# Retention then gated FFN on one core: the two stages interleaved, head pairs on half tiles, decays folded into v and y

## The chip, the core and the metric

The kernel runs on one core of one Trainium2 chip. The core has TensorE (PE, matmuls into PSUM; PEld is its weight load), VectorE (DVE), ScalarE (ACT), GpSimd (POOL) and SyncE (SP). Each runs its own instructions in the order written and waits on semaphores for the others. 16 DMA engines move data; a transfer is issued from the queue of SP, ACT or POOL, and an issue is an instruction like any other there. The metric is the device time of one execution in microseconds (us), lower is better.

## The reference

Batch 4, 8 heads, 768 positions, head size 64; then 3072 tokens of width 512 through an FFN of width 1536. Inputs and output are float32 in DRAM.

```python
gamma = 1.0 - 2.0 ** (-5.0 - np.arange(H))            # one decay per head
for t in range(S):
    state = gamma * state + einsum('bhd,bhe->bhde', k[:, :, t], v[:, :, t])
    y[:, :, t] = scale * einsum('bhd,bhde->bhe', q[:, :, t], state)
x = y.transpose(0, 2, 1, 3).reshape(B * S, H * D)
out = (1 / (1 + exp(-(x @ w_gate)))) * (x @ w_val) @ w_out
```

## The kernel before

It has two stages, one after the other; x stays on chip between them, transposed (features on partitions), in four tiles `xT` of 128 x 3072.

The retention stage loops over head `h`, and inside over batch entry `b`: 32 (head, batch) pairs. `issue_qkv_dma` (L84) loads q, k and v of the next pair with three transfers of 192 KB, issued from POOL, ACT and SP. ACT converts them to bf16 (L138). Six TensorE transposes (L147, L151) and twelve DVE copies make `qT` and `kT` with the 64 features on partitions. Then it walks six chunks of 128 positions. For each: scores `st_p` (L167, contraction over 64), a DVE product with the head's decay mask (L169), two matmuls that add into `yT_p` (L172 from the chunk, L173 from the state), an ACT copy into `xT` (L177), `cross_p` (L180), and a DVE step that decays the state and adds `cross_p` (L183). The state is a 64 x 64 bf16 tile in SBUF. All these work on one head, so they fill half of TensorE's rows or columns. The decay tables of each head are built at the head's start (ACT Exp with DVE and POOL steps).

The weights come in 20 transfers from POOL's queue (L135), two or three per head, converted to bf16 on the way.

The FFN stage loops over six tiles of 512 tokens. Per tile there are 12 pairs of `gate_p` and `val_p` (L199, L203: four matmuls of 512 columns each), a Sigmoid on ACT (L207) and a product on DVE (L208), and then four `out_p` of 12 matmuls each (L213), an ACT copy (L216) and a store from SP (L217).

A scheduler orders the instructions within each stage. PSUM pools of the retention stage are closed before those of the FFN open.

Of the kernel before, what the change touches and what calls it, by code (L numbers as in the profile page):

```python
# [10 lines left out]
F32 = mybir.dt.float32  # L11
BF16 = mybir.dt.bfloat16
I32 = mybir.dt.int32
# [5 lines left out]
def kernel(  # L19
# [15 lines left out]
    NCHUNK = S // C  # L35
    scale = 1.0 / math.sqrt(D)
    KT = D_MODEL // 128
    NFF = D_FF // 128
    MT = N_TOK // 512

    const = ctx.enter_context(tc.tile_pool(name="const", bufs=1))
    ident = const.tile([128, 128], BF16)
    make_identity(nc, ident)

    ii_free = const.tile([128, 128], I32)
    nc.gpsimd.iota(ii_free, pattern=[[1, 128]], base=0, channel_multiplier=-1)
    ii_col = const.tile([D, 128], I32)
    nc.gpsimd.iota(ii_col, pattern=[[1, 128]], base=0, channel_multiplier=0)
    ii_part = const.tile([128, 1], I32)
    nc.gpsimd.iota(ii_part, pattern=[[1, 1]], base=0, channel_multiplier=1)  # L50

    ii_free_f = const.tile([128, 128], F32)
    nc.vector.tensor_copy(ii_free_f, ii_free)
    ii_col_f = const.tile([D, 128], F32)
    nc.vector.tensor_copy(ii_col_f, ii_col)
    ii_part_f = const.tile([128, 1], F32)
    nc.vector.tensor_copy(ii_part_f, ii_part)

    xpool = ctx.enter_context(tc.tile_pool(name="xpool", bufs=1))
    xT_sb = [xpool.tile([128, N_TOK], BF16, tag=f"xT{kk}", name=f"xT{kk}")  # L60
             for kk in range(KT)]

    wpool = ctx.enter_context(tc.tile_pool(name="wpool", bufs=1))

    w_jobs = []
    def load_w_bf16(ap, tagbase, ktiles, width):
        tiles = []
        for kk in range(ktiles):
            tb = wpool.tile([128, width], BF16, tag=f"{tagbase}{kk}", name=f"{tagbase}{kk}")
            w_jobs.append((tb, ap[kk * 128:(kk + 1) * 128, :]))  # L70
            tiles.append(tb)
        return tiles

    wg_sb = load_w_bf16(moe_w_gate, "wg", KT, D_FF)
    wv_sb = load_w_bf16(moe_w_val, "wv", KT, D_FF)
    wo_sb = load_w_bf16(moe_w_out, "wo", NFF, D_MODEL)
    n_jobs = len(w_jobs)
    jobs_per_h = [(n_jobs * (i + 1)) // H - (n_jobs * i) // H for i in range(H)]
    job_idx = 0

    def issue_qkv_dma(attn, bb, hh):
        tfn = attn.tile([C, 3 * D * NCHUNK], F32, tag="qkvF")
        for i, (ap, eng) in enumerate([(q, nc.gpsimd), (k, nc.scalar), (v, nc.sync)]):
            eng.dma_start(  # L84
                out=tfn[:, i * D * NCHUNK:(i + 1) * D * NCHUNK].rearrange("s (c d) -> s c d", c=NCHUNK),
                in_=ap[bb, hh].rearrange("(c s) d -> s c d", c=NCHUNK))
        return tfn

    with tc.tile_pool(name="hmask", bufs=1) as hmask, \
         tc.tile_pool(name="attn", bufs=3) as attn, \  # L90
         tc.tile_pool(name="ps1", bufs=2, space=bass.MemoryType.PSUM) as ps1:
      tf_next = issue_qkv_dma(attn, 0, 0)
      for h in range(H):
          gamma = 1.0 - 2.0 ** (-5.0 - h)
          lg = math.log(gamma)
          cross_decay = gamma ** C

          b128 = hmask.tile([128, 1], F32, tag="b128")
          b64 = hmask.tile([D, 1], F32, tag="b64")

          mask_T = hmask.tile([128, 128], BF16, tag="mask")
          mtmp = hmask.tile([128, 128], F32, tag="mtmp")
          nc.vector.memset(b128, math.log(scale))
          nc.scalar.activation(mtmp, ii_free_f, AX.Exp, scale=lg, bias=b128)
          nc.gpsimd.affine_select(mtmp, mtmp, pattern=[[1, 128]], base=0,
                                  channel_multiplier=-1,
                                  compare_op=ALU.is_ge, fill=0.0)
          nc.vector.tensor_copy(mask_T, mtmp)

          lam = hmask.tile([D, S], BF16, tag="lam")  # L110
          ltmp = hmask.tile([D, 128], F32, tag="ltmp")
          nc.vector.memset(b64, math.log(scale) + lg)
          nc.scalar.activation(ltmp, ii_col_f, AX.Exp, scale=lg, bias=b64)
          for c in range(NCHUNK):
              nc.vector.tensor_copy(lam[:, c * C:(c + 1) * C], ltmp)  # L115

          eta = hmask.tile([128, 1], F32, tag="eta")
          nc.vector.memset(b128, (C - 1) * lg)
          nc.scalar.activation(eta, ii_part_f, AX.Exp, scale=-lg, bias=b128)

          xk = h // 2
          xoff = (h % 2) * D

          for b in range(B):
              state = attn.tile([D, D], BF16, tag="state")
              nc.gpsimd.memset(state, 0.0)

              tf = tf_next
              nb, nh = (b + 1, h) if b + 1 < B else (0, h + 1)
              if nh < H:  # L130
                  tf_next = issue_qkv_dma(attn, nb, nh)
              if b == 0:
                  for _ in range(jobs_per_h[h]):
                      tb_w, ap_w = w_jobs[job_idx]
                      nc.gpsimd.dma_start(out=tb_w, in_=ap_w)  # L135
                      job_idx += 1
              tb = attn.tile([C, 3 * D * NCHUNK], BF16, tag="qkvB")
              nc.scalar.activation(tb, tf, AX.Copy)  # L138
              qB = tb[:, 0:D * NCHUNK]
              kB = tb[:, D * NCHUNK:2 * D * NCHUNK]  # L140
              vB = tb[:, 2 * D * NCHUNK:3 * D * NCHUNK]

              qT = attn.tile([D, S], BF16, tag="qT")
              kT = attn.tile([D, S], BF16, tag="kT")
              for c2 in range(NCHUNK // 2):
                  qtp = ps1.tile([C, C], BF16, tag="tp", bufs=2)
                  nc.tensor.transpose(qtp, qB[:, c2 * C:(c2 + 1) * C], ident)  # L147
# [101 lines left out]
```

## Time and profile before

| what | value |
|---|---|
| median of 3 runs | 451.34 us (451.21 to 452.57) |
| profiled execution, span from first to last instruction | 449.5 us |
| TensorE busy | 391.6 us, 87% of the span |
| VectorE busy | 243.7 us, 54% |
| ScalarE busy | 152.7 us, 34% |
| GpSimd busy | 45.7 us, 10% |
| read from DRAM, written to DRAM | 28.31 MB, 6.29 MB |

The page gives no time of the profiled execution besides its span; the span is 1.84 us shorter than the median of the runs. TensorE's busy time counts overlapping matmuls by modelled ends, so 87% is no measure of how full its array is. The shares are averages over two stages that have different limits; the stages are told apart by reading stretches of the trace.

### The profile page before, as it was taken

Reading aid. Unit: us, or ns where it says so; the run is one execution under the profiler, and the core shown is the slowest. Engines: PE = TensorE matmul, PEld = TensorE weight load, DVE = VectorE, ACT = ScalarE, POOL = GpSimd, SP = SyncE. Lnnn points to the kernel's source line nnn. Section 1 sums busy time; section 2 is a strip of 40 time slices with the busy share of each in tenths; the row PEclk is TensorE's granted clock in tenths of the full one; section 3 lists DMA queues with packets and bytes.
Section 4 is the critical chain, followed back from the end, with each engine's and each line's share of the span. In section 5 each row is a group of like instructions: output and inputs, shape, how many; then the busy total and the mean of one; then the engine's idle time right before and its main releaser. Section 6 shows DMA issues by size and latency. Waiting matters only on the chain.

```text
span 449.5 us, 5825 instructions
## 1 busy us (share of the span) xinstructions
PE 391.6 (87%) x1824; PEld 188.0 (42%) x1824; DVE 243.7 (54%) x987; ACT 152.7 (34%) x346; POOL 45.7 (10%) x101
## 2 busy tenths in 40 slices
PE   1797987887896978878878899999999999999996
PEld 0343443443443434434444444444444444444442
DVE  3778787777878787877778634043132141330330
ACT  3333333334343343434242243233232332332321
POOL 5444111101101010111000000000000000000000
PEclk9999999999999999999999999999999999999999
DMA  9999633242423342242200000200200101101002
GB/s 186 225 235 219 137 88 71 58 102 53 105 55 79 79 96 64 64 95 53 53 3 1 1 1 0 77 18 0 95 0 25 71 0 48 47 2 70 23 1 93
DMA packets 58591, 30.26 MB, mean 67 GB/s; under 512 B 51392, under 2 KB 52928, under 8 KB 58560
## 3 DMA queue, kind: packets, MB, share of 16 engines
q0 software_dynamic: 4928, 11.01, 11.1%
q1 hardware_dynamic: 28544, 12.59, 10.6%
q10 hardware_dynamic: 25088, 6.29, 6.7%
q8 instruction: 14, 0.23, 0.2%
q14 instruction: 17, 0.14, 0.1%
HBM read 28.31 MB, written 6.29 MB: 77 GB/s over the span
## 4 chain that ended last, share of the span: by engine, by line
PE 57%; DVE 16%; issue 2%; ACT 1%; POOL 0%; ACTq 0%
PE gate_p L199 14%; PE val_p L203 14%; PE out_p L213 14%; PE yT_p L173 5%; PE st_p L167 4%; PE cross_p L180 3%; PE yT_p L172 3%; DVE qT L149 3%; DVE kT L153 3%; DVE kT L152 3%; DVE q_sc L156 2%; DVE qT L148 2%; DVE st L169 1%; DVE eta_v L158 1%; DVE lam L115 1%
## 5 line engine op out<-in xcount | busy, mean ns | idle before, releaser
L208 DVE TENSOR_TENSOR h<-gate_s,val_p 128x512 bf16<-128x512 f32 x72 | 49.5, 687 | 130.0 <-PE val_p L203 125.1
L177 ACT ACTIVATE xT<-yT_p 64x128 bf16<-64x128 f32 x192 | 51.4, 268 | 154.5 <-PE yT_p L173 154.2
L169 DVE TENSOR_TENSOR st<-st_p,mask_T 128x128 bf16<-128x128 f32 x192 | 55.4, 289 | 41.7 <-PE st_p L167 40.5
L199 PE MATMUL gate_p<-xT,wg 128*128 128x512 bf16 x288 | 74.7, 382 | 0.4 <-ACT xT L177 0.4
L203 PE MATMUL val_p<-xT,wv 128*128 128x512 bf16 x288 | 74.5, 382 | 0.0
L207 ACT ACTIVATE gate_s<-gate_p 128x512 f32<-128x512 f32 x72 | 43.0, 597 | 74.9 <-PE gate_p L199 74.9
L213 PE MATMUL out_p<-wo,h 128*128 128x512 bf16 x288 | 63.1, 379 | 0.0
L172 PE MATMUL yT_p<-st,tb 128*64 128x128 bf16 x192 | 57.8, 301 | 2.3 <-DVE st L169 0.5
L167 PE MATMUL st_p<-qT,kT 64*128 64x128 bf16 x192 | 54.7, 285 | 0.0
L180 PE MATMUL cross_p<-eta_v,tb 128*64 128x64 bf16 x192 | 42.0, 249 | 13.5 <-DVE eta_v L158 13.5
L173 PE MATMUL yT_p<-q_sc,state_new 64*64 64x128 bf16 x160 | 50.0, 313 | 0.0
L147 PE MATMUL qtp<-ident,tb 128*128 128x128 bf16 x96 | 27.6, 287 | 19.6 <-DVE qT L149 10.0
L151 PE MATMUL ktp<-ident,tb 128*128 128x128 bf16 x96 | 27.7, 288 | 18.5 <-DVE kT L153 18.3
L203 PEld LDWEIGHTS <-wv 128*128 128x128 bf16 x288 | 28.4, 99 | 34.6 <-issue 1.1
L199 PEld LDWEIGHTS <-wg 128*128 128x128 bf16 x288 | 28.3, 98 | 34.7 <-issue 1.1
L213 PEld LDWEIGHTS <-h 128*128 128x128 bf16 x288 | 28.2, 98 | 34.0
L138 ACT ACTIVATE tb<-tfn 128x1152 bf16<-128x1152 f32 x32 | 37.1, 1162 | 6.8 <-DMA tfn<-in_q_dram 4.2
L180 PEld LDWEIGHTS <-tb 128*64 128x64 bf16 x192 | 24.4, 128 | 30.4 <-issue 12.0
L183 DVE SCALAR_TENSOR_TENSOR state_new<-state_new,cross_p 64x64 bf16<-64x64 bf16 x160 | 32.4, 203 | 1.6 <-PE yT_p L173 0.8
L216 ACT COPY out_sb<-out_p 128x512 f32<-128x512 f32 x24 | 14.0, 585 | 53.5 <-PE out_p L213 53.5
L172 PEld LDWEIGHTS <-tb 128*64 128x64 bf16 x192 | 27.4, 143 | 10.2 <-DVE st L169 5.9
L84 POOL DMA_DIRECT2D tfn<-in_q_dram x32 | 26.8, 837 | 43.3 <-ACT xT L177 36.4
(40 smaller groups left out, 235.5 us busy)
## 6 DMA issues: line engine op xcount, KB each, us to landing
tfn<-in_k_dram ACTq DMA_DIRECT2D x32, 192.0 KB, 3.9
tfn<-in_v_dram SPq DMA_DIRECT2D x32, 192.0 KB, 3.4
tfn<-in_q_dram POOLq DMA_DIRECT2D x32, 192.0 KB, 4.4
out_dram<-out_sb SPq DMA_DIRECT2D x24, 256.0 KB, 2.0
wg<-in_moe_w_gate_dram POOLq DMA_DIRECT2D x4, 384.0 KB, 8.5
wv<-in_moe_w_val_dram POOLq DMA_DIRECT2D x4, 384.0 KB, 8.5
wo<-in_moe_w_out_dram POOLq DMA_DIRECT2D x12, 128.0 KB, 7.8
```

The lines of the kernel that those rows point to most:

```text
L138: nc.scalar.activation(tb, tf, AX.Copy)
L167: nc.tensor.matmul(st_p, k_dc, q_dc, start=True, stop=True)
L169: nc.vector.tensor_mul(st, st_p, mask_T)
L172: nc.tensor.matmul(yT_p, v_cd, st, start=True, stop=False)
L173: nc.tensor.matmul(yT_p, state, q_sc[:, c * C:(c + 1) * C], start=False, stop=True)
L177: nc.scalar.activation(xT_sb[xk][xoff:xoff + D, col0:col0 + C], yT_p, AX.Copy)
L180: nc.tensor.matmul(cross_p, k_cd, eta_v[:, c * D:(c + 1) * D], start=True, stop=True)
L199: nc.tensor.matmul(gate_p, wg_sb[kk][:, n1 * 128:(n1 + 1) * 128], xT_sb[kk][:, mt * 512:(mt + 1) * 512], start=(kk == 0), stop=(kk == KT - 1))
L203: nc.tensor.matmul(val_p, wv_sb[kk][:, n1 * 128:(n1 + 1) * 128], xT_sb[kk][:, mt * 512:(mt + 1) * 512], start=(kk == 0), stop=(kk == KT - 1))
L207: nc.scalar.activation(gate_s, gate_p, AX.Sigmoid)
L208: nc.vector.tensor_mul(hT[n1], gate_s, val_p)
L213: nc.tensor.matmul(out_p, hT[n1][:, sm * 128:(sm + 1) * 128], wo_sb[n1], start=(n1 == 0), stop=(n1 == NFF - 1))
```

## The change

The kernel is rewritten with its order given by hand. Work is organised by batch entry, and inside it by chunks of 128 positions of all eight heads at once (`load_chunk`: 128 x 8 x 64). q and k are converted to bf16 by the transfer itself and issued from POOL; v stays float32 and is issued from SP.

The decay gamma^(i-j) is split into gamma^-j, multiplied into v by POOL (`scale_v`, table `tabv`), and scale * gamma^i, multiplied into y by DVE (`taby`, the last line of `step_y`). What is between is plain causal attention without decay, so the masks are the same for all heads and the state is a plain sum: `z` adds up in one PSUM bank over the chunks of a batch entry.

Heads are handled in pairs. `step_t` transposes k and q of a chunk (8 matmuls, two heads each) and ACT copies all into SBUF at once. `step_s` makes the scores, 8 matmuls with a contraction of 64: even heads on rows 0 to 63 of the array, odd heads on rows 64 to 127, into two PSUM banks; DVE applies the causal mask to four heads at a time. `step_y` adds to `z` (4 matmuls), reads the masked copy of the earlier state (4 matmuls, not for the first chunk) and adds the products with the scores (8 matmuls into 64 output partitions each, even and odd heads on the two halves of the columns).

The FFN takes 768 tokens of one batch entry: 24 groups `up` (half of the tokens, four matmuls of 384 columns for the gate and four for the value) and 6 groups `down` (12 matmuls of 512 columns). The last loop emits the groups of entry b and between them, at most one after each group, the 18 steps of entry b+1. The steps of entry 0 come ahead of all groups. PSUM is split between five banks of attention, one each, and three that the FFN rotates through (`ff`).

The core of the diff (the removed loops stand in the functions above):

```diff
+    ctx.enter_context(tc.manual_schedule())
...
+    ld = ctx.enter_context(tc.tile_pool(name="ld", bufs=12))
+    at = ctx.enter_context(tc.tile_pool(name="at", bufs=2))
+    ffn = ctx.enter_context(tc.tile_pool(name="ffn", bufs=3))
+    pa = ctx.enter_context(tc.tile_pool(name="pa", bufs=1, space=bass.MemoryType.PSUM))
+    pf = ctx.enter_context(tc.tile_pool(name="pf", bufs=3, space=bass.MemoryType.PSUM))
...
+        vf[b, c] = ld.tile([C, H, D], F32, tag="vf", name="vf", bufs=8)
+        nc.gpsimd.dma_start(out=kn[b, c], in_=k[b, :, rows, :].rearrange("h s d -> s h d"))
+        nc.gpsimd.dma_start(out=qn[b, c], in_=q[b, :, rows, :].rearrange("h s d -> s h d"))
+        nc.sync.dma_start(out=vf[b, c], in_=v[b, :, rows, :].rearrange("h s d -> s h d"))
...
+    def load_gate_val(s):
+        cols = slice(s * 256, (s + 1) * 256)
+        for dst, src in ((wg, moe_w_gate), (wv, moe_w_val)):
+            nc.gpsimd.dma_start(out=dst[:, :, cols],
+                                in_=src.rearrange("(kk p) n -> p kk n", p=128)[:, :, cols])
...
+    def scale_v(b, c):
+        vs[b, c] = ld.tile([C, H, D], BF16, tag="vs", name="vs", bufs=8)
+        nc.gpsimd.tensor_tensor(vs[b, c], vf[b, c],
+                                tabv[:, c, :].unsqueeze(2).to_broadcast([C, H, D]), op=ALU.mult)
+
+    def step_t(b, c):
+        tp = pa.tile([128, 2 * NP, C], BF16, tag="tp", name="tp")
+        for i, src in enumerate((kn[b, c], qn[b, c])):
+            for p in range(NP):
+                nc.tensor.transpose(tp[:, i * NP + p, :],
+                                    src[:, 2 * p:2 * p + 2, :].rearrange("s h d -> s (h d)"), ident)
+        qkT[b, c] = at.tile([128, 2 * NP, C], BF16, tag="qkT", name="qkT")
+        nc.scalar.activation(qkT[b, c], tp, AX.Copy)
+
+    def step_s(b, c):
+        t = qkT[b, c]
...
+        for p in range(NP):
+            nc.tensor.matmul(sA[:, p, :], t[0:D, p, :], t[0:D, NP + p, :], start=True, stop=True)
+            nc.tensor.matmul(sB[:, p, :], t[D:128, p, :], t[D:128, NP + p, :], start=True, stop=True)
...
+        nc.vector.tensor_tensor(stA[b, c], sA, causal4, op=ALU.mult)
+        nc.vector.tensor_tensor(stB[b, c], sB, causal4, op=ALU.mult)
+
+    def step_y(b, c):
...
+                nc.tensor.matmul(zps[b][:, p, :],
+                                 kn[b, c][:, 2 * p:2 * p + 2, :].rearrange("s h d -> s (h d)"),
+                                 vs[b, c][:, 2 * p:2 * p + 2, :].rearrange("s h d -> s (h d)"),
+                                 start=(c == 0 and p == 0), stop=True, skip_group_check=True)
...
+                nc.tensor.matmul(y[:, p, :], zbd[b, c - 1][:, p, :], t[:, NP + p, :],
+                                 start=(p == 0), stop=False, skip_group_check=True)
+        for p in range(NP):
+            nc.tensor.matmul(y[0:D, p, :], vs[b, c][:, 2 * p, :], stA[b, c][:, p, :],
+                             start=(c == 0 and p == 0), stop=True, skip_group_check=True)
+            nc.tensor.matmul(y[D:128, p, :], vs[b, c][:, 2 * p + 1, :], stB[b, c][:, p, :],
+                             start=(c == 0 and p == 0), stop=True, skip_group_check=True)
+        if c < NCH - 1:
+            zbd[b, c] = at.tile([128, NP, C], BF16, tag="zbd", name="zbd")
+            nc.vector.tensor_tensor(zbd[b, c], zps[b], diag4, op=ALU.mult)
+        cols = slice(c * C, (c + 1) * C)
+        nc.vector.tensor_tensor(xT[b][:, :, cols], y, taby[:, :, cols], op=ALU.mult)
+
+    def attention(b):
+        steps = [lambda: step_t(b, 0), lambda: step_s(b, 0)]
+        for c in range(NCH):
+            if c + 1 < NCH:
+                steps.append(lambda c=c: step_t(b, c + 1))
+            steps.append(lambda c=c: step_y(b, c))
+            if c + 1 < NCH:
+                steps.append(lambda c=c: step_s(b, c + 1))
+        return steps
...
+        def up(n1, hf):
+            cols = slice(hf * HALF, (hf + 1) * HALF)
+            ps = []
+            for w in (wg, wv):
+                t = pf.tile([128, 512], F32, tag="ff", name="ff")
+                for kk in range(KT):
+                    nc.tensor.matmul(t[:, 0:HALF], w[:, kk, n1 * 128:(n1 + 1) * 128], xT[b][:, kk, cols],
+                                     start=(kk == 0), stop=(kk == KT - 1))
+                ps.append(t)
+            gs = ffn.tile([128, HALF], F32, tag="gs", name="gs")
+            nc.scalar.activation(gs, ps[0][:, 0:HALF], AX.Sigmoid)
+            nc.vector.tensor_tensor(hT[:, n1, cols], gs, ps[1][:, 0:HALF], op=ALU.mult)
...
+    for s in range(NFF // 2):
+        load_gate_val(s)
+    for s in range(4):
+        load_out(s)
+    for c in range(NCH):
+        scale_v(0, c)
+    for c in range(NCH):
+        load_chunk(1, c)
+    for step in attention(0):
+        step()
+    for b in range(B):
+        groups = ffn_groups(b)
+        steps = attention(b + 1) if b + 1 < B else []
...
+        for i, g in enumerate(groups):
+            g()
+            upto = -(-len(steps) * (i + 1) // len(groups))
+            while done < min(upto, len(steps)):
+                steps[done]()
+                done += 1
```

Three places in the new order matter below. The first is POOL's queue in the first part of the program. Before, loads of q (`tfn`) and of weights stood mixed, with small steps between:

```order
L84 DMA tfn<-in_q_dram 128x6x64
L135 DMA wg_85<-in_moe_w_gate_dram 128x1536
L105 AFFINE_SELECT mtmp<-mtmp 128x128 [waits Activation_49]
L135 DMA wg_86<-in_moe_w_gate_dram 128x1536
L84 DMA tfn<-in_q_dram 128x6x64
L84 DMA tfn<-in_q_dram 128x6x64 [waits DMAHW0_49,DMAHW1_49,DMASW0_49,Activation_49]
```

Now the twelve loads of k and q of entry 0 stand first, then all 16 loads of weights, then the six products that scale v of entry 0 (`vs`), and then the loads of entry 1. The end of the weights, with what follows:

```order
L70 DMA wv<-in_moe_w_val_dram 128x4x256 [waits DMASW7_49]
L74 DMA wo<-in_moe_w_out_dram 128x3x512 [waits DMASW0_49]
L74 DMA wo<-in_moe_w_out_dram 128x3x512 [waits DMASW1_49]
L74 DMA wo<-in_moe_w_out_dram 128x3x512 [waits DMASW2_49]
L74 DMA wo<-in_moe_w_out_dram 128x3x512 [waits DMASW3_49]
L118 TENSOR_TENSOR vs<-vf,tabv 128x512 [waits DMAHW0_49,Activation_49]
L118 TENSOR_TENSOR vs<-vf,tabv 128x512 [waits DMAHW1_49]
L118 TENSOR_TENSOR vs<-vf,tabv 128x512 [waits DMAHW2_49]
```

The names DMASW0 to DMASW7 are eight semaphores that POOL's transfers take in turn: each issue waits for the landing of the transfer eight places earlier. So the first `vs` moved behind the issue of the last `wo`, which waits for the landing of the eighth weight transfer (the fourth slice of `wv`).

The second place is TensorE in the attention of entry 0: the end of `step_t` of chunk 1, then `step_y` of chunk 0.

```order
L125 LDWEIGHTS qn
L125 MATMUL tp<-ident,qn 128x128
L149 LDWEIGHTS kn
L149 MATMUL z<-vs,kn 128x128 [waits Pool_49]
L149 LDWEIGHTS kn
L149 MATMUL z<-vs,kn 128x128
```

The first matmul on `z` waits for POOL's first `vs`, and all that TensorE has to do after it, the FFN included, stands behind it.

The third place is TensorE in the FFN. Before, a group of gate matmuls was followed by the value group and by nothing else:

```order
L203 LDWEIGHTS wv_91 [waits DMASW5_49]
L203 MATMUL val_p<-xT_80,wv_91 128x512
L203 LDWEIGHTS wv_92 [waits DMASW6_49]
L203 MATMUL val_p<-xT_81,wv_92 128x512
L199 LDWEIGHTS wg_85
L199 MATMUL gate_p<-xT_78,wg_85 128x512
```

Now a step of the next entry stands between two groups; here the end of `step_t` of entry 1, chunk 0, and the next group of entry 0:

```order
L125 LDWEIGHTS qn
L125 MATMUL tp<-ident,qn 128x128
L189 LDWEIGHTS wg
L189 MATMUL ff<-xT,wg 128x384 [waits DVE_49]
L189 LDWEIGHTS wg
L189 MATMUL ff<-xT,wg 128x384
```

TensorE has 1792 matmuls instead of 1824: 768 of 384 columns and 288 of 512 for the FFN (864 of 512 before, the same number of columns), and 736 of 128 columns for attention, 184 per batch entry (48 in `step_t`, 48 in `step_s`, and in `step_y` 20 on `z`, 20 with the earlier state and 48 with the scores).

## Rows read from the trace of the kernel before

**Rows 1.** Busy time of each engine in three stretches: retention, FFN, end

```profile
core 0: us, PE busy (x) PEld busy (x) DVE busy (x) ACT busy (x) POOL busy (x), PEclk, DMA share, GB/s
0.00:257.82 257.82, 203.53 (x960) 103.21 (x961) 194.20 (x915) 94.36 (x249) 45.72 (x101) 1.00 0.43 92
257.82:448.50 190.68, 188.05 (x864) 84.77 (x863) 49.47 (x72) 58.31 (x97) 0.00 (x0) 1.00 0.09 34
```

**Rows 2.** Chain that ended last, in order of time, two of its FFN pieces

```profile
280.12 10.36 PE out_p L213 x48
...
311.20 10.36 PE out_p L213 x48
```

**Rows 3.** Timeline of PE around the border of the two stages

```profile
256.37 0.26 PE L180 MATMUL cross_p<-eta_v,tb 128*64 128x64 bf16 x1
256.44 0.29 PE L172 MATMUL yT_p<-st,tb 128*64 128x128 bf16 x1
256.67 0.31 PE L173 MATMUL yT_p<-q_sc,state_new 64*64 64x128 bf16 x1
...
257.82 1.86 PE L199 MATMUL gate_p<-xT,wg 128*128 128x512 bf16 x4 [0.36 <-ACT xT L177]
259.48 1.64 PE L203 MATMUL val_p<-xT,wv 128*128 128x512 bf16 x4
260.96 1.03 PE L199 MATMUL gate_p<-xT,wg 128*128 128x512 bf16 x4
261.82 1.03 PE L203 MATMUL val_p<-xT,wv 128*128 128x512 bf16 x4
```

**Rows 4.** DMA queues from 100 to 133 us: packets, MB, share of 16 engines

```profile
q10 hardware_dynamic: 3136, 0.79, 10.6%
...
tfn<-in_k_dram ACTq DMA_DIRECT2D x4, 192.0 KB, 3.8
```

**Rows 5.** DMA from 2 to 33 us: busy tenths, queues, issues

```profile
DMA  8999999999999999999999999999999999999999
...
q0 software_dynamic: 1632, 4.65, 69.5%
q1 hardware_dynamic: 4980, 1.25, 24.1%
q10 hardware_dynamic: 4678, 1.18, 21.6%
...
tfn<-in_q_dram POOLq DMA_DIRECT2D x8, 192.0 KB, 7.4
```

**Rows 6.** Costliest groups of POOL: issues of loads, and a two-dimensional step

```profile
L84 POOL DMA_DIRECT2D tfn<-in_q_dram x32 | 26.8, 837 | 43.3 <-ACT xT L177 36.4 <-ACT tb L138 3.9 <-ACT eta L119 2.3
L135 POOL DMA_DIRECT2D wo<-in_moe_w_out_dram x12 | 6.4, 548 | 1.5 <-PE yT_p L173 0.6 <-DMA tfn<-in_v_dram 0.5 <-issue 0.3
...
L105 POOL TENSOR_SCALAR_AFFINE_SELECT mtmp<-mtmp 128x128 f32<-128x128 f32 x8 | 2.5, 313 | 1.7 <-ACT mtmp L104 1.7
```

**Rows 7.** Costliest groups of DVE and ACT on PSUM tiles

```profile
L208 DVE TENSOR_TENSOR h<-gate_s,val_p 128x512 bf16<-128x512 f32 x72 | 49.5, 687 | 130.0 <-PE val_p L203 125.1
...
L207 ACT ACTIVATE gate_s<-gate_p 128x512 f32<-128x512 f32 x72 | 43.0, 597 | 74.9 <-PE gate_p L199 74.9
...
L138 ACT ACTIVATE tb<-tfn 128x1152 bf16<-128x1152 f32 x32 | 37.1, 1162 | 6.8 <-DMA tfn<-in_q_dram 4.2
...
L216 ACT COPY out_sb<-out_p 128x512 f32<-128x512 f32 x24 | 14.0, 585 | 53.5 <-PE out_p L213 53.5
```

**Rows 8.** Timeline of PE, its first two matmuls

```profile
9.59 0.29 PE L147 MATMUL qtp<-ident,tb 128*128 128x128 bf16 x1 [9.59 <-ACT tb L138]
9.67 0.31 PE L151 MATMUL ktp<-ident,tb 128*128 128x128 bf16 x1
```

**Rows 9.** Timeline of PE at the end

```profile
438.81 7.07 PE L213 MATMUL out_p<-wo,h 128*128 128x512 bf16 x32
```

More of the change, by code (lines that the diff above doesn't have):

```diff
@@ L46 @@
[L46 to L87, printed above, removed]
@@ new lines @@
+    tabv = const.tile([128, NCH, H], F32, name="tabv")
+    for h in range(H):
+        nc.scalar.activation(tabv[:, :, h], tokv, AX.Exp, scale=-lg[h])
+    lgp = const.tile([128, NP], F32, name="lgp")
+    lsc = const.tile([128, 1], F32, name="lsc")
+    nc.vector.memset(lsc, math.log(scale))
+    for p in range(NP):
+        nc.vector.memset(lgp[0:D, p:p + 1], lg[2 * p])
+        nc.vector.memset(lgp[D:128, p:p + 1], lg[2 * p + 1])
+    diag = const.tile([128, 128], F32, name="diag")
+    nc.vector.memset(diag, 0.0)
@@ new lines @@
+    nc.vector.memset(diag[0:D, 0:D], 1.0)
+    nc.vector.memset(diag[D:128, D:128], 1.0)
+    taby = const.tile([128, NP, S], F32, name="taby")
+    for p in range(NP):
+        nc.scalar.activation(taby[:, p, :], toky, AX.Exp, scale=lgp[:, p:p + 1], bias=lsc)
+    causal4 = causal.unsqueeze(1).to_broadcast([128, NP, 128])
+    diag4 = diag.unsqueeze(1).to_broadcast([128, NP, 128])
+    for c in range(1, NCH):
+        load_chunk(0, c)
+    xT, vs, qkT, stA, stB, zps, zbd = {}, {}, {}, {}, {}, {}, {}
@@ L212 @@
             for n1 in range(NFF):
-                nc.tensor.matmul(out_p, hT[n1][:, sm * 128:(sm + 1) * 128], wo_sb[n1],
+                nc.tensor.matmul(o, hT[:, n1, sm * 128:(sm + 1) * 128], wo[:, n1, :],
                                  start=(n1 == 0), stop=(n1 == NFF - 1))
-            out_sb = ffn.tile([128, 512], F32, tag="out_sb")
-            nc.scalar.copy(out_sb, out_p)
-            nc.sync.dma_start(out=out[mt * 512 + sm * 128: mt * 512 + (sm + 1) * 128, :],
-                              in_=out_sb)
+            ob = ffn.tile([128, D_MODEL], F32, tag="ob", name="ob")
@@ new lines, in down @@
+            nc.scalar.copy(ob, o)
+            row = b * S + sm * 128
+            nc.sync.dma_start(out=out[row:row + 128, :], in_=ob)
+        return ([lambda n1=n1, hf=hf: up(n1, hf) for n1 in range(NFF) for hf in range(2)]
+                + [lambda sm=sm: down(sm) for sm in range(NCH)])
+    for s in range(NFF // 2):
[8 more added lines that the diff above has]
+        step()
@@ new lines @@
+    for b in range(B):
+        groups = ffn_groups(b)
+        steps = attention(b + 1) if b + 1 < B else []
+        if b + 1 < B:
+            for c in range(NCH):
+                scale_v(b + 1, c)
+        if b + 2 < B:
+            for c in range(NCH):
+                load_chunk(b + 2, c)
+        done = 0
+        for i, g in enumerate(groups):
[4 more added lines that the diff above has]
+                done += 1
```

158 lines of the change are left out of this document (46 added, 112 removed).

## The prediction

> **What bounds the kernel now.** I read the busy times by stretch first, then the chain that ended last, then TensorE's timeline at the border of the stages.
>
> The stretches [rows 1] divide the span of 449.5 us in two: 257.8 us of retention and 190.7 us of FFN. In the second TensorE is busy for 188.05 of 190.68 us, everything else waits for it. In the first no engine is full: TensorE 203.5 us and VectorE 194.2 of 257.8 us, and TensorE's count holds 960 matmuls of at most 128 columns whose modelled durations overlap. There the chain goes to and fro between a small matmul and a small VectorE step on one head.
>
> How full TensorE is in the FFN is seen in the chain [rows 2]: `out_p` of one tile of 512 tokens begins 31.08 us after that of the tile before (311.20 - 280.12). A tile is 144 matmuls of 512 columns, so 31.08 / 144 = 0.216 us each, or 0.054 us per 128 columns: this stage takes 6 x 31.08 = 186.5 us as long as TensorE has to do it. What can go is the retention stage.
>
> At the border [rows 3] a second thing shows. The first FFN matmuls come at 257.82 and 259.48, 1.66 us for four, 0.42 us each; from 260.96 to 261.82 it is 0.86 for four, 0.216 each. [...] The granted clock says 1.00 for the whole stretch [rows 1], so I go by the spacing: after the sparse work of the retention stage TensorE started slow, and about eight matmuls cost 0.2 us more each, 1.6 us.
>
> **The change, part by part.** The new kernel has three stretches: attention of entry 0 alone, the FFN of entries 0 to 2 with attention in between, and the FFN of entry 3.
>
> *Start, until the first scaled v.* POOL's first `vs` stands behind the issue of the last `wo`, which waits until 12 loads of k and q and 8 weight loads have landed. v runs beside them from SP's queue, eight loads at once. Prices: k loads at a quiet time take 10.6% of 16 engines in 33 us for four [rows 4], 0.106 x 33 / 4 = 0.87 us of all engines for 192 KB, so 1.17 us for 256 KB in the same runs of 256 bytes. Weights: from 2 to 33 us the engines are full [rows 5]; k and v moved 1.25 + 1.18 MB, q about 1.5 MB (eight issued, the last not yet done), 3.9 MB at 0.87 us per 0.197 MB make 17.3 us. The other 13.7 us carried the rest of POOL's queue, 4.65 - 1.5 = 3.15 MB of bf16 weights. A slice of 0.262 MB then takes 1.14 us. Sum: 20 x 1.17 + 8 x 1.14 = 32.5 us, from 2 us on: 34.5. I add 1.5 us for landing (an estimate: a 192 KB load lands 3.8 us after issue on quiet queues [rows 4], less 0.87 moving, and part of that overlaps the next), 0.55 us for the last issue and 1.25 us for the product (a POOL step of 128 columns takes 0.313 us [rows 6], four times that). First `vs` at 37.8 us. POOL's own issue time, 0.84 us for 768 runs [rows 6], hides under 1.17 us of moving and as much for v; without that cover it would still be less than the moving. What is not in the trace is a load that converts 256-byte runs to 128-byte ones. If only written bytes counted, twelve loads at half price save 7 us; if each cost double they add 14, and weights in runs of 1 KB instead of 6 KB at double price add 9. I take the price of the 256-byte row, since k and q still read such runs.
>
> *Attention of entry 0.* Steps for chunk 0 and the transposes of chunk 1 are done by then. After that each chunk needs four VectorE products of 128 x 512 from PSUM, at 0.687 us [rows 7] 2.75 us, and VectorE has to wait once per chunk for matmuls that stand behind `step_y`: some 0.65 us (six to eight matmuls of 128 columns at the slow level, 0.42 / 4 = 0.105 us each [rows 3]). 3.4 us per chunk; five such rounds and a first `step_y` of 12 matmuls at 0.105 (1.3 us) end at 37.8 + 17 + 1.3 = 56.1 us. ACT's copy of 1024 columns (1.16 us for 1152 [rows 7]) and POOL's 1.25 us run beside it. Bounds: 2.75 us per chunk (3 us less) and 5 us (8 more).
>
> *FFN matmuls.* The same columns, 186.5 us; plus the slow start of about eight matmuls, 1.6 us. The 192 additional instructions I take at nothing: at 384 columns the array works 0.16 us and the weight load, as now, lies beside it.
>
> *Attention between FFN groups.* 3 x 184 matmuls of 128 columns. The lower price is that of the FFN's columns, 0.054 us, with half-tile pairs at the same time at 0.027. The upper one is the spacing of small matmuls of unlike tile shape now, 0.23 us (L172 to L173, [rows 3]). In between lie neighbours of like shape: 0.08 us (L147 to L151 [rows 8]) and 0.07 (L180 to L172 [rows 3]). I take 0.08 for the 88 full-array ones and 0.054 for the 96 on half tiles, between 0.027 and 0.08: 7.0 + 5.2 us per entry. The shape of tile changes four times per chunk, into and out of the scores and into and out of the last part of `step_y`; from the rows a change costs between nothing and 0.23 - 0.054 = 0.18 us, and I take 0.12: 24 x 0.12 = 2.9 us. 15.1 us per entry, 45.3 for three; bounds 22 (7.3 per entry) and 127 (0.23 for each).
>
> [...] The rows show 0.23 us where the shape changes and 0.07 where it stays [rows 3]. [...]
>
> *What the FFN's groups cover.* In one entry's stretch of some 62 us VectorE has 24 FFN products and 24 attention products, 48 x 0.687 = 33 us at most; ACT 24 x 0.6 + 6 x 1.16 + 6 x 0.585 = 25 us; POOL 6 x 1.25 and 12 issues of about 0.95, 19 us [rows 6, 7]. Each product of VectorE delays the next FFN product behind it, and TensorE waits for its bank two groups later: after `step_s` it is two products, 1.4 us, behind which the next FFN product ends about 0.5 us before its bank is wanted. So I cost this at nothing, with a margin of only 0.5 us.
>
> *End.* The last matmul ended at 438.81 + 7.07 = 445.88 us, 3.6 us before the end of the span [rows 9]; copy and store are the same.
>
> Sum: 56.1 + 186.5 + 1.6 + 45.3 + 3.6 = 293.1 us of span; with the 1.84 us between span and median, 295 us. Against 451.34 this is a gain of 156 us; anything within 0.3% (1.4 us) would count as no change.
>
> **The rivals.**
>
> *Late loads.* Converting loads and short weight runs at double price: 14 + 9 us more, 318 us. For it: all early transfers run with full engines, nothing hides them. Against: k's price comes from runs of the same length.
>
> *Banks given back late.* The margin of 0.5 us is gone and each of the 54 interleaved steps costs TensorE one VectorE product, 54 x 0.69 = 37 us: 332 us. For it: three banks for two-bank groups; in-order queues. Against: VectorE is idle for half of the stretch.
>
> *Small matmuls at the old price*, 0.23 us each as when they stood alone [rows 3]: 127 instead of 45 us, 377 us. Against: those gaps lie between dependent matmuls of unlike shape, at the slow level.
>
> *Everything cheaper:* pairs truly at once and shape changes free (23 us less), or loads by written bytes (7 less): 265 to 281 us.
>
> *The other side: TensorE stays at the slow level while FFN and small matmuls alternate.* At 0.43 us per 512 columns the FFN takes 373 us and the attention between 91: 56 + 373 + 91 + 4 + 2 = 526 us, slower. It decides from about two thirds of the stretch on (156 of the 232 us it would add). For it: the stretch before 257.82, full of small matmuls, left TensorE slow [rows 3]. Against: there it was waiting between them; from 260.96 on, without waits, it is at the fast level to the end. [...]
>
> **How the numbers follow.** The forecast (281 to 311 us) has a chance of 0.44; everything cheaper (265 to 281) 0.18; late loads (311 to 325) 0.13; late banks (325 to 350) 0.13; small matmuls at the old price 0.07; slow level 0.04; a price below all bounds 0.01. The range leaves out the last three and the upper part of late banks: 265 to 338 us. The forecast's own range is 281 to 311. Only the slow level is slower; faster 0.955, same 0.005, slower 0.04.
>
> **What would show it.** The first matmul on `z` at about 38 us after a wait for POOL, and POOL's last weight issue just before it; the first FFN matmul at about 56 us; `out_p`-like groups of entry b and b+1 about 62 us apart for the first three and 47 us to the last; in that stretch next to no wait of TensorE for VectorE or ACT, and FFN matmuls 0.16 us apart. Wrong would be: a first `z` later than 45 us (loads), TensorE idle before FFN groups with VectorE as releaser (banks), spacing above 0.1 us between small matmuls of one step (their price), or FFN matmuls 0.32 us apart (the clock).

## The result and the profile after

The changed kernel takes 278.85 us (median of 4 runs, 277.96 to 279.18) against 451.87 us of the kernel before in runs beside it; the ratio is 0.617 with a 95% interval of 0.615 to 0.618. The forecast was 295 us with a range of 265 to 338. The profiled execution took 278.6 us, with a span of 276.9 us. One execution of experiment 4 (280.54 us, mean granted clock 0.982) was in a slower state of the chip and is left out of its median.

The stretches of the changed kernel, cut at the first matmul on `z`, the first FFN matmul and the first FFN matmul of each later entry (columns as in [rows 1]):

```profile
core 0: us, PE busy (x) PEld busy (x) DVE busy (x) ACT busy (x) POOL busy (x), PEclk, DMA share, GB/s
0.00:37.55 37.55, 2.98 (x25) 1.83 (x26) 2.17 (x14) 8.00 (x15) 25.69 (x40) 1.00 1.54 173
37.55:51.10 13.55, 11.16 (x161) 8.71 (x160) 12.25 (x20) 5.38 (x5) 11.20 (x13) 1.00 1.31 191
51.10:112.42 61.32, 58.95 (x452) 33.70 (x450) 27.97 (x48) 20.39 (x35) 37.42 (x41) 0.97 1.49 132
112.42:169.40 56.98, 56.98 (x450) 33.15 (x449) 27.20 (x47) 20.87 (x36) 6.25 (x6) 1.00 0.22 56
169.40:226.36 56.96, 56.96 (x449) 33.11 (x448) 27.20 (x47) 20.87 (x36) 0.00 (x0) 1.00 0.08 29
226.36:276.90 50.54, 46.90 (x265) 25.74 (x263) 13.27 (x24) 15.86 (x31) 0.00 (x0) 1.00 0.10 37
```

Where [rows 1] had 257.8 us in which TensorE never had enough to do, there are now 37.55 us before the first `z`, nearly all of them waiting, 13.55 us of attention alone, and then stretches with TensorE busy throughout. An entry with interleaved attention takes 56.97 us, the last one without 46.9 us to its last matmul, so the attention of one entry costs 10.1 us of TensorE.

Who waited for whom, in the list of waits of the whole span (engine and line, whom it waited for: us in total, times, longest), three of the rows in which TensorE waits:

```profile
PE z L149 <- POOL vs L118: 23.7, 1, 23.7
...
PE tp L125 <- DMA kn<-in_k_dram: 8.0, 2, 7.3
...
PE tp L125 <- DMA qn<-in_q_dram: 4.1, 3, 1.7
...
```

All of TensorE's waits lie before 56 us; between 60 and 226 us TensorE waited for nobody. The long one is the wait for the first scaled v. POOL's timeline shows what stood ahead of it:

```profile
30.30 0.74 POOL L70 DMA_DIRECT2D wv<-in_moe_w_val_dram  x1 [0.61 <-DMA wv<-in_moe_w_val_dram]
...
35.65 0.77 POOL L74 DMA_DIRECT2D wo<-in_moe_w_out_dram  x1 [0.58 <-DMA wv<-in_moe_w_val_dram]
36.44 6.04 POOL L118 TENSOR_TENSOR vs<-vf,tabv 128x512 bf16<-128x512 f32 x6
42.43 0.95 POOL L59 DMA_DIRECT2D kn<-in_k_dram  x1
```

The last `wo` was issued at 35.65 us, when a `wv` had landed, and the six products followed. From 30.30 to 35.65 us each issue waits 0.58 to 0.61 us for one landing, and the issues come 1.34 us apart. The loads of entry 1 stood behind them, and TensorE met that after its first FFN group (timeline of PE; the number in brackets is the idle time before):

```profile
51.10 0.82 PE L189 MATMUL ff<-xT,wg 128*128 128x384 bf16 x4
51.76 0.81 PE L189 MATMUL ff<-xT,wv 128*128 128x384 bf16 x4
53.20 0.40 PE L125 MATMUL tp<-ident,kn 128*128 128x128 bf16 x4 [0.63 <-DMA kn<-in_k_dram]
55.34 0.58 PE L125 MATMUL tp<-ident,qn 128*128 128x128 bf16 x4 [1.74 <-DMA qn<-in_q_dram]
55.70 1.49 PE L189 MATMUL ff<-xT,wg 128*128 128x384 bf16 x4
56.98 1.49 PE L189 MATMUL ff<-xT,wv 128*128 128x384 bf16 x4
```

Two waits of 2.4 us together, and behind them a group at half speed: four matmuls in 1.28 us instead of 0.66. Here the granted clock shows it too; the stretch from 56 to 58 us reads

```profile
56.00:58.00 2.00, 2.00 (x8) 0.91 (x6) 0.00 (x0) 1.51 (x2) 0.52 (x2) 0.50 1.71 157
```

with a granted clock of 0.50 (the column PEclk), after TensorE had been idle for some 3.5 us in pieces from 49 us on (0.48, 0.21, 0.38, 0.63 and 1.74). Before the change matmuls at the border of the stages were slowed by as much, 0.42 us each and then 0.216 [rows 3]; there the granted clock reads 1.00.

How small matmuls go in the steady stretch, from the timeline of PE (`step_y` of one chunk between two FFN groups `down`):

```profile
100.05 0.39 PE L149 MATMUL z<-vs,kn 128*128 128x128 bf16 x4
100.27 0.39 PE L156 MATMUL y<-qkT,zbd 128*128 128x128 bf16 x4
100.59 0.24 PE L159 MATMUL y<-stA,vs 128*64 128x128 bf16 x1
100.59 0.24 PE L161 MATMUL y<-stB,vs 128*64 128x128 bf16 x1
...
100.93 2.76 PE L199 MATMUL ff<-wo,hT 128*128 128x512 bf16 x12
```

Four full matmuls take 0.22 us (100.05 to 100.27), 0.056 each. The pair on half tiles starts at the same time to 0.01 us, and four pairs with the change of shape behind them take 0.34 us (100.59 to 100.93). From the start of the last full four to the first pair it is 0.32 us: 0.22 of work and 0.10 for the change of shape. The spacing of unlike neighbours in [rows 3], 0.23 us, was half as much again as the 0.10 + 0.056 of here. It was a price of the slow level, as this run shows it: at the start of the attention of entry 0, where four transposes still take 0.40 us, unlike neighbours stand 0.25 us apart, and a small matmul is listed with 0.28 to 0.31 us, much as in [rows 3] (0.26 to 0.31), against 0.22 to 0.24 for these shapes in the steady stretch:

```profile
38.38 0.31 PE L161 MATMUL y<-stB,vs 128*64 128x128 bf16 x1
38.63 0.28 PE L135 MATMUL sA<-qkT 64*128 64x128 bf16 x1
```

The granted clock reads 1.00 in that stretch, as it does in [rows 1], so the level is read from the spacing: four full matmuls take 0.40 us at the slow level and 0.22 at the fast one.

### The profile page after: what moved, and what is told of

Same layout as the page of the kernel before. It is cut to its first block, busy times and chain, and to the rows that moved or that the text cites. A ratio compares the mean times of both kernels' runs of the same rounds, so it can differ in the third digit from the quotient of the medians.

```text
span 276.9 us, 4474 instructions
## 1 busy us (share of the span) xinstructions
PE 233.9 (84%) x1792; PEld 136.2 (49%) x1792; DVE 110.1 (40%) x200; ACT 91.4 (33%) x158; POOL 80.6 (29%) x98
## 4 chain that ended last, share of the span: by engine, by line
PE 79%; DMA 12%; POOL 7%; issue 1%; ACT 0%; POOLq 0%; ACTq 0%
PE ff L189 46%; PE ff L199 23%; DMA qn<-in_q_dram 9%; DMA wg<-in_moe_w_gate_dram 4%; PE tp L125 3%; POOL vs L118 2%; PE y L159 2%; PE sA L135 2%; POOL kn L59 2%; PE y L156 1%; PE z L149 1%; POOL qn L60 1%; POOL wo L74 1%; POOL wv L70 1%; POOL toky L84 0%
## 5 line engine op out<-in xcount | busy, mean ns | idle before, releaser
L194 DVE TENSOR_TENSOR hT<-gs,ff 128x384 bf16<-128x384 f32 x96 | 53.1, 554 | 75.2 <-PE ff L189 57.6
L189 PE MATMUL ff<-xT,wg 128*128 128x384 bf16 x384 | 79.1, 329 | 0.0
L189 PE MATMUL ff<-xT,wv 128*128 128x384 bf16 x384 | 78.8, 328 | 0.0
L193 ACT ACTIVATE gs<-ff 128x384 f32<-128x384 f32 x96 | 47.0, 489 | 78.6 <-PE ff L189 47.8
L199 PE MATMUL ff<-wo,hT 128*128 128x512 bf16 x288 | 64.4, 379 | 0.0
L189 PEld LDWEIGHTS <-wv 128*128 128x128 bf16 x384 | 37.8, 98 | 25.2 <-issue 0.7
L199 PEld LDWEIGHTS <-hT 128*128 128x128 bf16 x288 | 27.3, 98 | 31.9
L128 ACT ACTIVATE qkT<-tp 128x1024 bf16<-128x1024 bf16 x24 | 24.6, 1023 | 48.0 <-PE tp L125 48.0
L118 POOL TENSOR_TENSOR vs<-vf,tabv 128x512 bf16<-128x512 f32 x24 | 24.4, 1042 | 45.4 <-PE y L161 17.3
L59 POOL DMA_DIRECT2D kn<-in_k_dram x24 | 22.0, 915 | 6.0 <-DMA kn<-in_k_dram 3.6
L60 POOL DMA_DIRECT2D qn<-in_q_dram x24 | 21.6, 902 | 5.3 <-DMA qn<-in_q_dram 3.6
L139 DVE TENSOR_TENSOR stA<-sA,causal 128x512 bf16<-128x512 f32 x24 | 16.4, 683 | 16.5 <-PE sB L136 16.5
L167 DVE TENSOR_TENSOR xT<-y,taby 128x512 bf16<-128x512 f32 x24 | 16.4, 682 | 14.5 <-PE y L161 14.5
## 6 DMA issues: line engine op xcount, KB each, us to landing
wg<-in_moe_w_gate_dram POOLq DMA_DIRECT2D x6, 256.0 KB, 10.1
```

The costliest lines, as they stand in the source:

```text
L59: nc.gpsimd.dma_start(out=kn[b, c], in_=k[b, :, rows, :].rearrange("h s d -> s h d"))
L60: nc.gpsimd.dma_start(out=qn[b, c], in_=q[b, :, rows, :].rearrange("h s d -> s h d"))
L118: nc.gpsimd.tensor_tensor(vs[b, c], vf[b, c], tabv[:, c, :].unsqueeze(2).to_broadcast([C, H, D]), op=ALU.mult)
L128: nc.scalar.activation(qkT[b, c], tp, AX.Copy)
L139: nc.vector.tensor_tensor(stA[b, c], sA, causal4, op=ALU.mult)
L167: nc.vector.tensor_tensor(xT[b][:, :, cols], y, taby[:, :, cols], op=ALU.mult)
```

## The experiments

In each the edit is against the changed kernel unless it says otherwise; times are medians, beside 278.85 us.

**1. No interleaving.**

```diff
-        done = 0
-        for i, g in enumerate(groups):
-            g()
-            upto = -(-len(steps) * (i + 1) // len(groups))
-            while done < min(upto, len(steps)):
-                steps[done]()
-                done += 1
+        for g in groups:
+            g()
+        for step in steps:
+            step()
```

> The 18 steps of entry b+1 come after all 30 FFN groups of entry b instead of between them; nothing else is changed. Theory 1 (most of the gain is the cheaper attention, not the interleaving): an entry's attention by itself takes as long as that of entry 0 did, 13.5 us from its first z to its last y, instead of the 10.2 us that it adds between FFN groups: 3 x 3.3 = 10 us more, less some 4 us because the first FFN no longer waits for k and q of entry 1: about 285 us. Rival (the interleaving carries the gain, since attention alone is bound by waits as the retention stage was): over 310 us.

294.66 us (ratio to the kernel before 0.652, interval 0.650 to 0.653): between the two, 10 us above theory 1 and 15 below the rival. Its chain in order of time gives the period of an entry and why theory 1 was short:

```profile
115.79 31.31 PE ff L189 x192
...
158.16 4.50 PE ff L199 x20
163.30 0.94 ACT qkT L128
...
167.12 0.68 DVE stA L139
...
178.60 32.61 PE ff L189 x192
```

178.60 - 115.79 = 62.8 us, so 16 us of attention after 46.9 of FFN. The steps run at VectorE's pace from 167.12 on, and before that some 4.5 us go to filling the row: transposes, ACT's copy, scores and first masks. Theory 1 counted from the first `z` and left these out: 3 x (16 - 13.5) = 7.5 us of its 10. Most of the rest is TensorE at the slow level behind the attention: in the chain the `up` groups of the first, third and fourth FFN take 33.07, 32.61 and 32.99 us, those of the second 31.31. The granted clock is 0.96 from 51 to 98 us, 0.91 from 163 to 181 and 0.97 from 228 us on, and 1.00 from 98 to 163; four matmuls of 384 columns take 1.28 us at 52.48 and 0.65 from 55.73 us on. Interleaving is worth 16 us in all, against 157 us that remain without it. Most of the gain is the cheaper attention: 16 us by itself per entry, where retention took 257.8 / 4 = 64 us [rows 1]. Which part of the rebuilding makes it cheaper (eight heads per instruction, pairs, the decay taken out, conversion by the transfer) no run separates.

**2. Pairs apart.**

```diff
         for p in range(NP):
             nc.tensor.matmul(sA[:, p, :], t[0:D, p, :], t[0:D, NP + p, :], start=True, stop=True)
+        for p in range(NP):
             nc.tensor.matmul(sB[:, p, :], t[D:128, p, :], t[D:128, NP + p, :], start=True, stop=True)
```

and the same split in the last part of `step_y`.

> The score matmuls and the products with the scores are issued four even heads first, then four odd ones, so that neighbours use the same half of the array. Theory 1 (the two halves of a pair run at the same time, 0.056 us per pair): eight matmuls more in a row per chunk, 8 x 0.056 = 0.45 us, in 18 interleaved chunks 8 us, about 287 us. Rival (the half-tile matmuls are bound by their issue, or the halves overlap whatever the order): within 1 us of 279.

280.05 us (278.03 to 281.53), no difference beyond the spread of the runs, as the rival had it. The timeline shows its second case: the matmuls on the second half, which stand behind all four of the first in TensorE's order, start among them.

```profile
103.67 0.23 PE L135 MATMUL sA<-qkT 64*128 64x128 bf16 x1
103.69 0.23 PE L137 MATMUL sB<-qkT 64*128 64x128 bf16 x1
103.74 0.22 PE L135 MATMUL sA<-qkT 64*128 64x128 bf16 x1
103.75 0.22 PE L137 MATMUL sB<-qkT 64*128 64x128 bf16 x1
```

So the order did not separate the halves, and the total could not tell whether the second one costs time. That needed the next run.

**3. Odd scores left out.** The four score matmuls of the odd heads go, and the even heads' scores stand for both.

```diff
-        sB = pa.tile([128, NP, C], F32, tag="sB", name="sB")
...
-            nc.tensor.matmul(sB[:, p, :], t[D:128, p, :], t[D:128, NP + p, :], start=True, stop=True)
...
-        nc.vector.tensor_tensor(stB[b, c], sB, causal4, op=ALU.mult)
+        nc.vector.tensor_tensor(stB[b, c], sA, causal4, op=ALU.mult)
```

> The score matmuls of the odd heads are left out, and the scores of the even heads are used for both, so the output is not the reference's. Theory 1 (the two halves of a pair run at the same time): the even halves take as long alone, less than 1 us gained, 278 to 279 us. Rival (each half-tile matmul takes its own 0.056 us): 18 interleaved chunks x 4 x 0.056 = 4 us less and 1 us in entry 0, 274 us.

278.32 us (276.89 to 279.46). Spans differ by the slow group at 56 us, which the profile of this run does not have, so I compare the steady stretch, by the first `down` piece of two successive entries in the chain (first this run, then the changed kernel):

```profile
93.64 4.91 PE ff L197 x22
...
150.59 4.91 PE ff L197 x22
```

```profile
95.03 5.18 PE ff L199 x24
...
152.00 5.18 PE ff L199 x24
```

They stand 56.95 us apart, and 56.97 with all matmuls. 24 matmuls less per entry saved 0.02 us: the second half of a pair of scores costs nothing here.

```profile
101.97 0.40 PE L134 MATMUL sA<-qkT 64*128 64x128 bf16 x4
102.30 2.98 PE L197 MATMUL ff<-wo,hT 128*128 128x512 bf16 x13
```

Four even halves alone take 0.33 us with the change of shape, as eight did (103.63 to 103.96 in the changed kernel). So it is not the issue of instructions that binds either. For the pairs on the two halves of the columns no such run was made; that they run together is read from their equal starts (100.59 above).

**4. An extra product on VectorE.**

```diff
         nc.vector.tensor_tensor(stB[b, c], sB, causal4, op=ALU.mult)
+        if b > 0:
+            nc.vector.tensor_tensor(stB[b, c], sB, causal4, op=ALU.mult)
```

> VectorE does the mask product of the odd heads twice in entries 1 to 3, so 18 times 0.6 us more in the interleaved stretch. Theory 1 (the FFN's banks are back before TensorE wants them, with the half microsecond of slack that the prediction gave or more): 0 to 2 us more, 281 us at most. Rival (late banks: each microsecond of VectorE between groups is one of TensorE's): 18 x 0.6 = 11 us more, 290 us.

276.73 us (275.76 to 277.66), VectorE 121.8 us busy instead of 110.1, and the same 56.97 us per entry (93.46 to 150.43 in the chain). The rival of late banks is excluded for one more product per chunk.

**5. Scaling first.** The loop over `scale_v(0, c)` stands ahead of the weight loads.

> The six products that scale v of entry 0 are moved ahead of all weight loads on POOL; all loads keep their order. Theory 1 (the start is set by the transfers that stand ahead of k and q of entry 1, which land when they land): the first z comes at about 16 us instead of 37.6, but TensorE then waits for k and q of entry 1 after the first FFN group; only POOL's six products (6 us) no longer stand ahead of those loads, so 3 to 6 us less, 273 to 276 us. Rival (the wait for the first scaled v is itself the loss): 13 us less or more, 266 us at most.

283.81 us (ratio to before 0.628, interval 0.627 to 0.629): neither, it is slower. The first `z` came at 15.64 us as expected, the first FFN group at 34.27, and then (waits of TensorE; timeline of POOL):

```profile
PE tp L125 <- DMA kn<-in_k_dram: 30.6, 3, 22.7
```

```profile
36.07 0.74 POOL L70 DMA_DIRECT2D wg<-in_moe_w_gate_dram  x1 [1.37 <-DMA wg<-in_moe_w_gate_dram]
38.27 0.74 POOL L70 DMA_DIRECT2D wv<-in_moe_w_val_dram  x1 [1.46 <-DMA wv<-in_moe_w_val_dram]
```

k of entry 1 was there at 59.35 us instead of 53.20. Theory 1 had the right place of the wait and wrongly took the landings as fixed: weight slices now came 2.2 us apart, 1.34 in the changed kernel. DMA from 20 to 45 us shows SP's queue (q1) with 1.65 MB, in the changed kernel 0.22:

```profile
q0 software_dynamic: 8108, 2.80, 94.8%
q1 hardware_dynamic: 6554, 1.65, 49.5%
```

Those are some six loads of v of later entries (256 KB each): their buffers came free with the early products.

**6. Scaling first, v behind.** As 5, and

```diff
-        nc.sync.dma_start(out=vf[b, c], in_=v[b, :, rows, :].rearrange("h s d -> s h d"))
+        (nc.sync if b == 0 else nc.gpsimd).dma_start(out=vf[b, c], in_=v[b, :, rows, :].rearrange("h s d -> s h d"))
```

> As the run with the scaling first, but v of entries 1 to 3 is loaded from POOL's queue behind the weights instead of from SP's queue. Theory 2 (with the scaling first, v of entries 1 and 2 was let loose early and took its share of the engines from the weights and from k and q of entry 1): weight slices land 1.3 us apart again instead of 2.1, k of entry 1 lands at about 47 us, total 268 to 272 us. Rival (POOL's six products left the transfer queue empty, which set k of entry 1 back): k of entry 1 at about 59 us as before, 283 us.

275.65 us (ratio to before 0.610, interval 0.608 to 0.611). POOL's issues of weights, now free of v, are 1.35 us apart again, and k of entry 1 is there at 49.39 us, 10 us earlier than in 5:

```profile
30.32 0.74 POOL L70 DMA_DIRECT2D wv<-in_moe_w_val_dram  x1 [0.56 <-DMA wv<-in_moe_w_val_dram]
31.66 0.74 POOL L74 DMA_DIRECT2D wo<-in_moe_w_out_dram  x1 [0.60 <-DMA wg<-in_moe_w_gate_dram]
```

```profile
49.39 0.61 PE L125 MATMUL tp<-ident,kn 128*128 128x128 bf16 x4 [18.79 <-DMA kn<-in_k_dram]
```

That bears theory 2 out in mechanism; the total is 4 us above its range. k came 2 us later than theory 2 had it, the two groups of four behind it (50.77 to 53.3 us) ran at half speed, 1.28 us each instead of 0.66, and there was a wait that theory 2 did not have, since on POOL the scaling of v of entry 1 stands behind all its loads (waits of TensorE; the longer one is for POOL's product of 61.61 to 62.67 us):

```profile
PE z L149 <- POOL vs L118: 4.3, 2, 2.6
```

The rival's empty queue exists too, but is short: DMA's busy tenths from 20 us on begin 9405 in steps of 0.6 us.

**7. Output weights last.** The loop over `load_out` stands behind `load_chunk(1, c)`.

> The four loads of the output weights are moved behind the scaling of v of entry 0 and the loads of entry 1 on POOL. Theory 1: the first scaled v comes when the last gate and value slice is issued, 5.3 us earlier, and k and q of entry 1 land before the first FFN group is over, which saves the 2.4 us of waits and some 2 us at the lower clock after them: about 9.5 us less, 269 us. Rival (only the order ahead of the scaling counts, the wait for entry 1 stays): 5 us less, 274 us.

275.22 us (ratio to before 0.608, interval 0.607 to 0.610). The first `z` came 5.9 us earlier (31.70), the first FFN group 6.1 us earlier (45.02). k was there in time; q was still 1 us late, the groups on both sides of it ran at the slow level (45.94 and 49.24 us; 1.28 us for four matmuls, 0.66 from 52.39 us on), and a new wait of 1.9 us arose at the first `z` of entry 1, since the scaling of its v now stood behind the output weights. Theory 1 was 6 us too hopeful and the rival 1 us off, though not by its reason alone: the order ahead of the scaling gave 6 us at the first FFN group, and what came behind it took 2.5 of them back, less wait for k and q against the new wait and the slow groups.

**8. All loads in order of need**, the version that follows from 5 to 7. The line that loads v is as in 6; the loads of chunks 1 to 5 of entry 0, of the weights and of entry 1 and the scaling of entry 0 leave their old places, and the new order is (in part)

```diff
+    load_chunk(0, 1)
+    load_chunk(0, 2)
     for c in range(NCH):
         scale_v(0, c)
+        if c + 3 < NCH:
+            load_chunk(0, c + 3)
+        elif c + 3 == NCH:
+            load_gate_val(0)
+            load_gate_val(1)
+            load_chunk(1, 0)
     for step in attention(0):
         step()
+    for c in range(NCH):
+        if c + 2 < NCH:
+            load_gate_val(c + 2)
+        else:
+            load_out(2 * (c + 2 - NCH))
+            load_out(2 * (c + 2 - NCH) + 1)
+        if c + 1 < NCH:
+            load_chunk(1, c + 1)
+        scale_v(1, c)
...
-        if b + 1 < B:
+        if 0 < b < B - 1:
             for c in range(NCH):
                 scale_v(b + 1, c)
```

> All loads from POOL in the order in which they are needed: chunks of entry 0 with the scaling of v two chunks behind, two slices of gate and value weights, then per chunk of entry 1 a slice of weights, its k, q and v, and the scaling; output weights last; v of entries 1 to 3 from POOL. Theory 1 (start set by the transfers that stand ahead, steady stretch by TensorE): the attention of entry 0 goes at the pace of its loads, 3.2 us per chunk, and ends at about 28 us, no wait for entry 1 later: 28 + 3 x 57 + 46.8 + 3.6 = 249 us of span, 251 us. Rival (the engines are full for the first 55 us whatever the order, and the first FFN entry only gets slower): 265 us or more.

252.11 us (251.63 to 252.81; ratio to the kernel before 0.557, interval 0.556 to 0.559): 27 us faster than the changed kernel, and 1 us from the expectation. Its stretches (columns as in [rows 1]):

```profile
0.00:28.49 28.49, 14.52 (x185) 10.55 (x185) 14.51 (x34) 13.38 (x20) 27.61 (x39) 1.00 1.62 165
28.49:85.45 56.96, 56.71 (x448) 33.13 (x449) 27.89 (x48) 20.31 (x35) 49.68 (x57) 1.00 1.52 191
...
142.40:199.40 57.00, 56.74 (x446) 33.13 (x448) 27.21 (x47) 20.90 (x36) 0.00 (x0) 1.00 0.08 29
199.40:250.10 50.70, 46.81 (x263) 25.71 (x263) 13.32 (x24) 15.89 (x31) 0.00 (x0) 1.00 0.10 37
```

The first entry takes 56.96 us although the DMA engines are full beside it (a share of 1.52, 191 GB/s), so its loads no longer hold TensorE up. 221.6 us of the 250.1 are now the FFN, with attention between for the first three entries. Of the 28.5 us ahead the loads set only the first part: the first `z` comes at 14.13 us after waits for k and q, and one round takes 3.6 us (transposes at 12.56 and 16.11 us), near the 3.2 that I expected from the loads; from the scores at 18.94 us on the rounds take VectorE's 2.4 us (the next scores at 21.33, 23.70 and 26.10). So the start came out as expected (28) with another limit for most of it.

## Why the prediction was right, and where its terms were off

The measured 278.85 us lie in the stated range, but 16 us below the 295 of the forecast and below the forecast's own 281 to 311: they fall to the group "everything cheaper", which had a chance of 0.18. The order of events and what bounds each stretch were right, the sizes were too high, nearly all on one side. Of that group's conditions one came true, pairs at once (0.01 us apart at 100.59 us); a change of shape is not free (0.10 us), and the loads together took what I had priced. The group's 23 us are also more than what it names: 3 x 96 x 0.027 for the pairs and 8.6 for the changes make 16.4, and the rest is the full matmuls at 0.054 us.

The order of the sum against the profile after:

| term | predicted, us | measured, us |
|---|---|---|
| until the first scaled v reaches TensorE | 37.8 | 37.55 |
| attention of entry 0 | 18.3 | 13.55 |
| FFN matmuls | 186.5 | 187.5 (4 x 46.87) |
| FFN matmuls at the slow level | 1.6 | 2.0 (61.32 - 56.97 - 2.4) |
| wait for k and q of entry 1 | 0 | 2.4 |
| attention between FFN groups | 45.3 | 30.3 (3 x 10.1) |
| end | 3.6 | 3.6 |
| span | 293.1 | 276.9 |

*The start* was right in place and price, and so was what set it: POOL's queue, where the first product stood behind the issue of the last `wo`. That it came out to 0.3 us is in part luck, since single prices were off and made up for each other: a weight slice took 1.34 us and not 1.14, and a POOL product 1.0 and not 1.25. Late loads as a rival (318 us) did not come. What I missed is what is late next: the loads of entry 1 stand behind those same products, and that cost 2.4 us of waits and the slow group. I had costed the slow level once, at the start of the FFN; it came one group later, since TensorE was at the fast level already in the attention of entry 0 (four transposes take 0.40 us from 39.17 us on and 0.23 from 41.96).

*Attention of entry 0* was priced by the duration of VectorE's product, 0.687 us [rows 7]. Back to back they start 0.60 us apart, though each lasts 0.68:

```profile
43.47 0.68 DVE L165 TENSOR_TENSOR zbd<-z,diag 128x512 bf16<-128x512 f32 x1
44.07 0.68 DVE L167 TENSOR_TENSOR xT<-y,taby 128x512 bf16<-128x512 f32 x1
44.67 0.68 DVE L139 TENSOR_TENSOR stA<-sA,causal 128x512 bf16<-128x512 f32 x1
45.27 0.68 DVE L140 TENSOR_TENSOR stB<-sB,causal 128x512 bf16<-128x512 f32 x1
```

So a round is 4 x 0.60 = 2.4 us without a wait of VectorE; I had 2.75 and a wait of 0.65 on top. The first two rounds, with TensorE still slow, took 2.5 and 2.8 us (the second with a wait of 0.31), and the last product waited 0.47. This step failed in size: the five rounds took 2.5 us each on average, below even the lower bound of 2.75.

*Attention between groups* was the largest miss, 15 us, and of size too. Full matmuls cost 0.056 us, not 0.08, as cheap as the FFN's columns; pairs on half tiles run together (shown by run 3 for the scores; no row of the kernel before has such a pair, and 0.054 was my choice), 0.028 each and not 0.054; the change of shape costs 0.10, and 0.12 was close. For three entries that is 6.3, 7.5 and 1.4 us. By these, 88 x 0.056 + 96 x 0.028 + 24 x 0.10 = 10.0 us per entry against 10.1 measured. The rows that I chose for the middle, neighbours of like shape in the kernel before [rows 3, 8], were not prices of a dense stream at the fast level: in the stretches that these rows come from, no more than two matmuls of like shape stand in a row, and they run at the slow level (listed with 0.26 to 0.31 us each).

*Cover.* That VectorE, ACT and POOL are hidden held, with more slack than the 0.5 us I gave: an extra 0.6 us of VectorE per chunk cost nothing (run 4). *The slow level as a rival* did not come: with interleaved small matmuls the granted clock stayed at 1.00 from 60 us to the end. What I had put against that rival, the fast level without waits in [rows 3], held here: from 60 to 226 us TensorE waited for nobody, and at 169.39 and 226.36 us four matmuls of 384 columns take 0.65 us. The rival's 0.43 us per 512 columns was an estimate beside the 0.42 of [rows 3]; the slow group at 56 us, 1.28 us for four of 384 columns, comes to the same 0.43.

Where the 173 us came from: retention's 257.8 us became 37.55 us before the first `z`, 13.55 of attention alone, 30.3 between FFN groups and some 4.4 of waits and slow matmuls, 86 us in all. Run 1 splits it: without interleaving 157 us of gain are there already, by the rebuilt attention as a whole; interleaving adds 16.

What stays open: whether the half tiles matter much by themselves. Run 3 shows that the second half is free for the scores; if it is so for the other pairs too, 96 halves per entry cost 2.7 us instead of 5.4. A version with full tiles was not tried. And why the slow group at 56 us did not come in runs 3 and 4, where the waits for k and q after the first group were 0.5 to 0.7 us shorter, is seen but not explained.

## What to carry to other kernels

When several engines feed one in-order queue, read what stands ahead of the first instruction that the bottleneck waits for, and then what stands behind it: here moving only the waited-for product forward made the kernel slower (283.81 us against 278.85), since it let loose a transfer on another queue that took the engines from what was needed next. Loads in the order of need, nearly all on one queue, gave 27 us where single moves gave 3 to 4 or lost 5. Price a repeated instruction by the start-to-start time of a dense row of them, not by its duration (VectorE's product here 0.60 us against 0.68), and if the trace has no dense row, widen the range downward as well.

## What the runs showed that I had not expected

In run 2 matmuls on the two halves of the array did not start in the order of the program: four on rows 0 to 63 followed by four on rows 64 to 127 started alternately, the second kind 0.01 to 0.02 us behind the first (103.67 and 103.69, 103.74 and 103.75). Transfers of one queue slowed those of another: with some six loads of v beside them, weight slices went from 1.34 to 2.2 us each (run 5). And TensorE's half clock (granted 0.50 from 56 to 58 us) after 2.4 us of waits was worth more than half of the waits themselves: the eight FFN matmuls behind them took 2.56 us in the chain instead of 1.30. The spans of runs 4 and 3, without that group and with less wait, were 1.9 and 1.7 us shorter (275.0 and 275.2 against 276.9).
